# Two-token rows for the first loads, idle matmuls in planned waits, and last stores by SP

## The chip, the cores and the metric

One Trainium2 chip, one core of it. Its engines are TensorE (PE in the profiles, PEld for its weight loads), VectorE (DVE), ScalarE (ACT) and GpSimd (POOL); SP only issues transfers. A line of events gives start and length in us, the engine, the line of the kernel, the operation and what it writes and reads, and in brackets the engine's idle time before it and what ended it. The metric is the device time of one launch in microseconds (us), as the median of several runs. A profile of one launch gives a span, in nearly all launches some 1.7 to 2 us shorter than that launch's time because it counts from the first to the last instruction. A run over 1.5% above the fastest of the same kernel is called slow.

## The reference

A gated linear attention over 768 tokens (4 batches, 8 heads, head size 48), followed by an MLP over the 3,072 resulting rows of 384 values:

```python
f = 1.0 / (1.0 + np.exp(-f_logit))
for t in range(S):                                    # S = 768
    state = f[:, :, t, :, None] * state + np.einsum('bhd,bhe->bhde', k[:, :, t], v[:, :, t])
    y[:, :, t] = np.einsum('bhd,bhde->bhe', q[:, :, t], state)
x = y.transpose(0, 2, 1, 3).reshape(B * S, H * D)
h = x @ w_in                                          # 384 -> 2048
out = (h * sigmoid(h)) @ w_out                        # 2048 -> 384
```

## The kernel before

The sequence is cut into six chunks of 128 tokens. A *unit* is one chunk of one batch with all eight heads, so that there are 24 units, numbered (m, j): m is half a chunk (two batches), j one of the two batches. In a unit ScalarE makes Exp and Ln of f, TensorE the cumulative sum `cs` by a triangular matrix, ScalarE the factors `ia` and `a`, GpSimd `ki = k*ia`, VectorE `qg = q*a`. Then TensorE transposes both (`t_ps`), multiplies them (`a_ps`), VectorE masks (`atm`), and TensorE makes the outputs `y_ps` and the state update `d_ps`. The result, transposed, is `xT`, and the MLP (`h_ps`, then Silu to `hT`, then `o_ps`) runs on it.

Nothing is scheduled by hand. A small planner in the kernel simulates all engines with a duration for each task and writes the instructions out in the order that it finds. It is told how long a load takes, and how loads by SP and weights by GpSimd share the DMA engines while both run. What the planner believes decides the order of every engine, and that order is fixed before the launch.

```python
def load(m, j, name):                                 # one unit, one tensor: 128 tokens x 8 heads, rows of 48 fp32 = 192 B
    g, b = m // 2, m % 2 * HB + j
    t = ld.tile([C, H, D], F32, name=f"{name}_ld")    # 8 buffers
    src = SRC[name].rearrange("b h s d -> s (b h) d")[g * C:(g + 1) * C, b * H:(b + 1) * H]
    nc.sync.dma_start(out=t, in_=src)
# ...
def load_w_in(n):                                     # weights, fp32 to bf16 on the way, by GpSimd
    nc.gpsimd.dma_start(out=w_in_sb[:, :, n:n + 512], in_=w_in_src[:, :, n:n + 512])
# ... in the planner: idle matmuls, only ahead of the first MLP matmul
if e == "PE" and filler is not None and until in left:
    at = max(free.get(e, 0.0), 1.0)
    while start - at > 0.6:
        self.order.append((at, filler))
        at += 0.165 if at > 4.5 else 0.33
# ...
COPY, STORE = "ACT", "POOL"                           # all 24 stores by GpSimd
BEFORE = {0: ["ki1.0"]}                               # the first weights are issued behind ki of unit (1, 0)
SHARE = (0.25, 0.75)                                  # loads : weights while both flow, as the planner believes
```

The weights are 6.3 MB, and TensorE can do no MLP without their first piece. Idle matmuls (`w_ps`) multiply zeros; they are there to keep TensorE's clock up.

## Time and profile before

| | before |
|---|---|
| median of 3 runs, range | 204.23 us (203.98 to 205.19) |
| span of the profiled run, its TensorE clock | 203.2 us, 0.975 |
| first MLP matmul, last matmul | 22.25 us, 198.07 us |
| from the last matmul to the end | 5.1 us |
| half-clock stretches in the trace after 8 us | 12.2 to 15.6 and 70.3 to 77.1 us |

The order of events at the end:

```profile
198.15 0.48 ACT L424 COPY o_sb<-o_ps 128x384 f32<-128x384 f32 x1 [1.47 <-PE o_ps L418]
198.92 0.54 POOL L432 DMA_DIRECT2D out_dram<-o_sb  x1 [1.41 <-ACT o_sb L424]
```

The last copy ends at 198.63; GpSimd issues the store for 0.54 us and the span ends at 203.2.

### The profile page before, as it was taken

How to read it: one execution, taken by the hardware profiler on the slowest of the kernel's cores; microseconds unless marked ns; L12 is line 12 of the kernel's file. 1: busy time of each engine (PE TensorE's matmuls, PEld its weight loads, DVE VectorE, ACT ScalarE, POOL GpSimd, SP SyncE). 2: the span in 40 equal slices, each digit the busy share in tenths (PEclk: the TensorE clock that was granted, in tenths of full speed). 3: DMA queues.
4: the chain of work that ended last, by engine and by line, in shares of the span. 5: the costliest groups of instructions: out<-in, count | busy, mean ns of one | idle time of the engine just before them, and what ended most of it. 6: DMA issues, size and time to landing. Idle time of an engine off the chain costs nothing.

```text
span 203.2 us, 5048 instructions
## 1 busy us (share of the span) xinstructions
PE 186.7 (92%) x2076; PEld 139.1 (68%) x2076; DVE 112.5 (55%) x214; ACT 130.6 (64%) x244; POOL 59.0 (29%) x90
## 2 busy tenths in 40 slices
PE   7788899997999489979999999999999999999990
PEld 3445799554876258658768888667778889865650
DVE  3478650048784956589989940399999750000000
ACT  4446488646898664987798779996346568911110
POOL 5339600135241421192047110473520000012221
PEclk9979999999999959999999999999999999999999
DMA  7999999999999999999999997021110000002111
GB/s 133 187 187 167 170 188 184 197 194 286 189 184 209 214 182 188 180 225 217 175 198 220 205 176 110 2 79 42 39 54 27 3 0 3 0 30 75 68 69 71
DMA packets 105110, 27.06 MB, mean 133 GB/s; under 512 B 100352, under 2 KB 103936, under 8 KB 105088
## 3 DMA queue, kind: packets, MB, share of 16 engines
q1 hardware_dynamic: 99840, 18.88, 58.5%
q0 software_dynamic: 5248, 7.87, 16.2%
q8 instruction: 16, 0.26, 0.6%
q14 instruction: 6, 0.05, 0.1%
HBM read 25.17 MB, written 4.72 MB: 147 GB/s over the span
## 4 chain that ended last, share of the span: by engine, by line
PE 37%; issue 27%; DMA 12%; SPq 9%; DVE 7%; POOL 4%; ACT 2%; POOLq 0%; DVEq 0%; ACTq 0%
PE h_ps L403 14%; DMA q_ld<-in_q_dram 11%; PE o_ps L418 10%; SPq L227 9%; PE t_ps L312 3%; POOL out_dram L432 3%; PE h_ps L388 2%; PE a_ps L324 2%; DVE st L379 2%; DMA f_ld<-in_f_logit_dram 2%; DVE qg L288 2%; POOL ki L285 1%; PE y_ps L344 1%; DVE sd L376 1%; PE y_ps L340 1%
## 5 line engine op out<-in xcount | busy, mean ns | idle before, releaser
L418 PE MATMUL o_ps<-w_out_sb,hT 128*128 128x384 bf16 x384 | 68.4, 326 | 0.4 <-DMA w_out_sb<-in_moe_w_out_dram 0.4
L403 PE MATMUL h_ps<-xT,w_in_sb 128*128 128x256 bf16 x432 | 53.5, 279 | 0.0
L412 ACT ACTIVATE hT<-h_ps 128x512 bf16<-128x512 f32 x72 | 42.8, 597 | 16.3 <-PE h_ps L403 13.7
L418 PEld LDWEIGHTS <-hT 128*128 128x128 bf16 x384 | 36.0, 98 | 22.1 <-issue 0.6
L403 PEld LDWEIGHTS <-w_in_sb 128*128 128x128 bf16 x432 | 41.5, 100 | 6.0 <-issue 0.2
L285 POOL TENSOR_TENSOR ki<-k_ld,ia 128x384 bf16<-128x384 f32 x24 | 24.4, 1018 | 53.5 <-ACT ia L277 41.3
L288 DVE TENSOR_TENSOR qg<-q_ld,a 128x384 bf16<-128x384 f32 x24 | 21.3, 886 | 29.9 <-ACT a L282 18.8
L331 DVE TENSOR_TENSOR atm<-a_ps,triu 128x512 bf16<-128x512 f32 x48 | 30.9, 684 | 7.2 <-PE a_ps L324 6.9
L432 POOL DMA_DIRECT2D out_dram<-o_sb x24 | 13.6, 567 | 57.5 <-ACT o_sb L424 55.1
L424 ACT COPY o_sb<-o_ps 128x384 f32<-128x384 f32 x24 | 11.4, 477 | 23.4 <-PE o_ps L418 23.4
L291 POOL CAST vb<-v_ld 128x384 bf16<-128x384 f32 x22 | 12.9, 593 | 28.8 <-DMA v_ld<-in_v_dram 19.8
L277 ACT ACTIVATE ia<-cs 128x384 f32<-128x384 f32 x24 | 11.8, 492 | 11.4 <-PE cs L272 11.4
L388 PE MATMUL h_ps<-xT,w_in_sb 128*128 128x128 bf16 x288 | 17.7, 219 | 1.3 <-DVE xT L362 0.8
L317 DVE COPY qk<-t_ps 128x1024 bf16<-128x1024 bf16 x24 | 16.4, 682 | 4.4 <-PE t_ps L312 4.4
L258 ACT ACT_TABLE_LOAD x14 | 18.0, 1283 | 1.0 <-PEq L560 0.7
L388 PEld LDWEIGHTS <-w_in_sb 128*128 128x128 bf16 x288 | 16.4, 98 | 2.0 <-issue 1.0
L396 ACT ACTIVATE hT<-h_ps 128x512 bf16<-128x512 f32 x24 | 14.0, 597 | 5.1 <-PE h_ps L388 4.1
L351 DVE CAST y<-y_ps 128x384 bf16<-128x384 f32 x24 | 13.3, 554 | 7.2 <-PE y_ps L344 6.9
L265 ACT ACTIVATE f_ld<-f_ld 128x384 f32<-128x384 f32 x24 | 12.5, 522 | 6.1 <-DMA f_ld<-in_f_logit_dram 6.1
L379 DVE TENSOR_TENSOR st<-sd,al 48x192 bf16<-48x192 f32 x32 | 13.6, 425 | 0.8
L312 PE MATMUL t_ps<-ident,qg 128*128 128x128 bf16 x96 | 9.8, 226 | 3.6 <-DVE qg L288 3.5
L266 ACT ACTIVATE lf<-f_ld 128x384 bf16<-128x384 f32 x24 | 12.5, 523 | 0.8
(41 smaller groups left out, 182.2 us busy)
## 6 DMA issues: line engine op xcount, KB each, us to landing
f_ld<-in_f_logit_dram SPq DMA_DIRECT2D x24, 192.0 KB, 4.5
k_ld<-in_k_dram SPq DMA_DIRECT2D x24, 192.0 KB, 4.6
q_ld<-in_q_dram SPq DMA_DIRECT2D x24, 192.0 KB, 4.5
v_ld<-in_v_dram SPq DMA_DIRECT2D x24, 192.0 KB, 4.7
out_dram<-o_sb POOLq DMA_DIRECT2D x24, 192.0 KB, 2.2
w_in_sb<-in_moe_w_in_dram POOLq DMA_DIRECT2D x4, 384.0 KB, 8.3
w_out_sb<-in_moe_w_out_dram POOLq DMA_DIRECT2D x4, 384.0 KB, 16.4
```

Source lines behind the costliest of these rows:

```text
L227: nc.sync.dma_start(out=t, in_=src)
L258: nc.scalar.preload_act_table_set(tables[name])
L285: nc.gpsimd.tensor_mul(ki[m % 4][:, j, :, 0:D], loaded[m, j, "k"], ias[m, j])
L288: nc.vector.tensor_mul(qg[m % 4][:, j, :, 0:D], loaded[m, j, "q"], aas[m, j])
L317: nc.vector.tensor_copy(qkT[m, j], t_ps[m, j])
L331: nc.vector.tensor_mul(atm[m, j][:, r], att[m, j][:, r], triu[:, None, :].to_broadcast([C, NP, C]))
L379: nc.vector.tensor_mul(st[b][lo:lo + D, :, r * D:(r + 1) * D], src[lo:lo + D, :, r * D:(r + 1) * D], alast[m][lo:lo + D, j, :, None].to_br ...
L388: nc.tensor.matmul(h_ps[:, i], w_in_sb[:, kk, (n + i) * 128:(n + i + 1) * 128], xT[m][:, kk, j], start=(kk == 0), stop=(kk == KT - 1))
L403: nc.tensor.matmul(h_ps[:, i], w_in_sb[:, kk, (n + i) * 128:(n + i + 1) * 128], xT[m][:, kk].rearrange("p b c -> p (b c)"), start=(kk == 0 ...
L412: nc.scalar.activation(hT[m][:, n:n + 2, :], hs[m, n], AF.Silu)
L418: nc.tensor.matmul(os[m, j], hT[m][:, i, j * C:(j + 1) * C], w_out_sb[:, i, :], start=(i == 0), stop=(i == NT - 1))
L432: eng.dma_start(out=out[r0:r0 + C, :], in_=osb[m, j])
```

## The change

It has three parts. First, the loads of chunk 0 (m = 0 and 1) fetch two neighbouring tokens in one row of 384 B. Partition p then holds two tokens, 64 partitions are one batch, and a unit becomes half the heads of two batches; the cumulative sum, scores, outputs, updates and state are rewritten for that layout, and a unit now needs both loads of a pair. Second, idle matmuls may fill any wait that the planner foresees (over 0.4 us), not only those ahead of the MLP, as long as a buffer in PSUM, where TensorE writes its results, is free. Third, the last 8 stores are issued by SP and not by GpSimd. To make room, the other loads have six buffers and no longer eight. With new durations and ranks the planner also finds another order.

```diff
-            if e == "PE" and filler is not None and until in left:
+            if e == "PE" and filler is not None:
                 at = max(free.get(e, 0.0), 1.0)
-                while start - at > 0.6:
+                size, taken = self.pools["h"]
+                while start - at > self.slack:                       # 0.4
+                    if len(taken) >= size:
+                        if taken[-size] not in self.freed or self.freed[taken[-size]] > at:
+                            break
                     self.order.append((at, filler))
 ...
+    WIDE = (0, 1)
 ...
+        if m in WIDE:
+            if j == 0:
+                loaded[m, name] = singles.tile([C, H, 2, D], F32, name=f"{name}_w{m}")
 ...
+            src = SRC[name][b].rearrange("h (s i) d -> s h (i d)", i=2)[g * 64:(g + 1) * 64]
+            nc.sync.dma_start(out=loaded[m, name][64 * j:64 * (j + 1)].rearrange("p h i d -> p h (i d)"), in_=src)
+            return
 ...
+        if m in WIDE:                                                # cumulative sum: three matmuls for one
+            nc.tensor.matmul(dst, upto, src[:, 0:1].to_broadcast([C, 2, 4, D]), start=True, stop=False, ...)
+            nc.tensor.matmul(dst[:, 0], before, src[:, 1], start=False, stop=True, ...)
+            nc.tensor.matmul(dst[:, 1], upto, src[:, 1], start=False, stop=True, ...)
 ...
-        eng = {"ACT": nc.scalar, "POOL": nc.gpsimd, "SP": nc.sync}[STORE]
+        eng = nc.sync if m >= LATE else nc.gpsimd                    # LATE = 8
 ...
-                add(U(name, m, j), "LD", 1.07 + 1.5 * first, do(load, m, j, name), [user] if m >= 4 else [])
+            add(U(name, m, j), "LD", (0.78 if m in WIDE else 1.07) + 1.5 * first, do(load, m, j, name), ...)
 ...                                                                  # scores, outputs, updates, state: likewise rewritten
```

## The prediction

> **What bounds the kernel now.** I read the page first, then the busy time by stretch, the chain of waits, the order of events at the start and around the stalls.
>
> The page's 40 slices (5.08 us each; a digit is tenths busy):
>
> ```profile
> PE   7788899997999489979999999999999999999990
> PEclk9979999999999959999999999999999999999999
> DMA  7999999999999999999999997021110000002111
> ```
>
> The reader is to see three regimes. TensorE is full from slice 17 on; before that it has holes and two slices of reduced clock (slices 2 and 14, counted from 0); and the DMA engines are busy without a break until about 127 us. The same by stretch (length, then busy us and instruction count of each engine, clock, DMA share, GB/s):
>
> ```profile
> 0.00:22.25 22.25, 17.76 (x155) 9.90 (x155) 14.16 (x37) 10.78 (x21) 12.90 (x25) 0.92 1.22 168
> 22.25:41.55 19.30, 18.82 (x264) 15.68 (x264) 4.94 (x11) 13.16 (x22) 2.45 (x3) 1.00 1.21 184
> 41.55:100.00 58.45, 52.02 (x639) 39.36 (x640) 43.11 (x74) 43.85 (x83) 20.20 (x30) 0.94 1.12 205
> 100.00:198.07 98.07, 98.07 (x1022) 74.17 (x1019) 50.31 (x94) 62.32 (x118) 22.95 (x32) 1.00 0.37 76
> ```
>
> From 100 us to TensorE's last matmul at 198.07 nothing can be won except by less matmul work, and the change removes none. So time can come only from the fill (first MLP matmul at 22.25), from the stretch 41.55 to 100 (6.4 us idle and a clock of 0.94), and from the 5.1 us after the last matmul.
>
> The fill is paced by loads. In the order of events the loads follow each other on the SP queue every 1.05 us (0.99 us issue plus 0.04), and ScalarE begins on the four f tiles, loads 1, 5, 9 and 13, at 3.69, 7.91, 12.13 and 16.34: 4.22 us for four loads of 192 KB. Then the weights come, and the loads all but stop:
>
> ```profile
> 16.42 3.26 POOL L247 DMA_DIRECT2D w_in_sb<-in_moe_w_in_dram  x4
> 19.35 6.58 SPq L227 DMA_DIRECT2D q_ld<-in_q_dram  x1
> 22.25 1.51 PE L388 MATMUL h_ps<-xT,w_in_sb 128*128 128x128 bf16 x24 [0.53 <-DMA w_in_sb<-in_moe_w_in_dram]
> 25.98 5.72 SPq L227 DMA_DIRECT2D v_ld<-in_v_dram  x1
> 31.74 5.16 SPq L227 DMA_DIRECT2D f_ld<-in_f_logit_dram  x1
> 36.94 4.13 SPq L227 DMA_DIRECT2D k_ld<-in_k_dram  x1
> 40.93 0.56 DVE L288 TENSOR_TENSOR qg<-q_ld,a 128x384 bf16<-128x384 f32 x1 [10.79 <-DMA q_ld<-in_q_dram]
> ```
>
> Weights are issued at 16.42, once ki of the third unit is done, and the MLP starts at 22.25 on the first piece, 5.8 us later. While the 6.3 MB of fp32 weights flow (to about 41 us) a load takes some 5.5 us instead of 1.05. The q tile of chunk 1, issued at 19.35, is used at 40.93. This hurts little before the change, because TensorE has weights-paced MLP work of the first two unit pairs in that stretch.
>
> The third place to look is the largest hole:
>
> ```profile
> 66.78 2.22 DVE L379 TENSOR_TENSOR st<-sd,al 48x192 bf16<-48x192 f32 x2
> 67.33 1.00 POOL L285 TENSOR_TENSOR ki<-k_ld,ia 128x384 bf16<-128x384 f32 x1
> 69.64 0.40 PE L312 MATMUL t_ps<-ident,qg 128*128 128x128 bf16 x4 [2.06 <-DVE qg L288]
> ```
>
> Two state multiplies, 0.72 us elsewhere, took 2.22 us beside GpSimd's multiply; TensorE waited 2.06 us, and then ran slow: 12 matmuls of 256 columns took 2.67 us in the chain at 73.91, against 1.33 us at 91.44.
>
> **What the Trainium skill says.**
> - "DMA: Bandwidth & Descriptors", How a descriptor splits into AXI transactions: reads go in 256 B pieces from 256 B boundaries, 32 B beats; Why small descriptors are slow adds about 3 cycles per packet. A 192 B row then averages 9 beats plus 3 (the four alignments give 6, 12, 10, 8), a 384 B row 14 plus 3. Estimate: 17/(2 x 12) = 0.71 of the time, 1.05 x 0.71 = 0.75 us a load. No row of 384 B is in this trace.
> - "SBUF — State Buffer", Door 1: 64 partitions of one half reach 8 of the 16 ports. Each new load writes just 64 partitions, so if that binds, half of 435 GB/s gives 0.90 us (estimate). The planner's new number is 0.78, between the two. I take 0.78.
> - "DMA: Bandwidth & Descriptors", Queues, rings and completion order: each DMA engine takes turns between queues packet by packet. The trace agrees: 192 B rows lose badly to weight packets, 5.5 us against 1.05.
> - "TensorE: Matmul & The Clock Gate", Part 1: too little activity in a window of about 3.4 us halves the clock. The trace agrees: 12 matmuls at double time right after the 2.06 us hole.
>
> **The change part by part.**
>
> *Loads of chunk 0.* Sixteen loads at 0.78 instead of 1.05: 16 x 0.27 = 4.3 us less DMA time. But a unit is now half the heads of two batches, so both loads of a pair are needed: first f data at 3.69 - 1.05 + 2 x 0.78 = 4.2, later by 0.5. The third and fourth units need loads 9 and 10: 2.64 + 10 x 0.78 = 10.4 instead of 12.1 and 16.3.
>
> *Issue of the weights.* Still behind ki of the third unit. From 10.4: ScalarE now does both f pairs of Exp and Ln first (4 x 0.52), then ia (0.49), GpSimd ki (1.0), with 0.15 for hand-overs: 14.2 against 16.42, so -2.2. First weights 5.8 us later: MLP from 20.1.
>
> *What the new order puts into the weights' time.* Compared instruction by instruction, the new order on VectorE puts qg of chunk 1's first unit ahead of the masking of the last chunk-0 unit, and on TensorE its transposes after the second 24 MLP matmuls. Before, TensorE did all 192 MLP-in matmuls of chunk 0 and 36 MLP-out ones ahead of those transposes. So q and then v of chunk 1 are now needed while weights flow. First weight packets come about 1.6 us after issue, at 15.8; by then 16 x 0.78 = 12.5 us of loads from 1.65 are done, and 1.6 loads of chunk 1. The rest of k and all of q, 1.4 loads at 5.5 us and the about 3 us dead at the start of the weights, bring q to about 26.5 and v to about 32.5. TensorE would come to the transposes at about 24.4 (second weight piece), so it waits 3 us there and again for v: outputs of that unit at about 33.5, then a free run of 144 MLP matmuls (8.0 us) to 42. Counting finished matmul work at 0.0555 us per 128 columns and 0.1625 per 384 (chain: 36 in 2.01, 8 in 1.30), the new kernel at 42 has done about what the old one had at 40. The 4.3 us won are given back and 2 us more.
>
> *Stretch 42 to 100.* Here the old one loses some 12 us against its matmul work: idle, the halved clock, bubbles. At 42 the new one holds the hidden activations of three units instead of two and a reserve of 80 MLP-out matmuls (13 us), and the loads of the next units come 4 us earlier, so the holes at 48 to 51 should go. The hole at 66 comes from VectorE and GpSimd in each other's way and can come anywhere. I put the loss at 6 to 7 us, -5.5.
>
> *Extra matmul work.* Cumulative sums as three matmuls (0.33 for 0.165), scores as 16 instead of 8 (+0.33), outputs and updates with twice the columns (+0.25): 0.75 us x 4 units = 3 us, all in the fill, where TensorE waits. Idle matmuls go from 44 to 49, all but two before the MLP outputs begin; 5 x 0.165 us is nothing, and they cover planned waits only, not the wait for q.
>
> *Last stores by SP.* ScalarE's last copy ends at 198.63, GpSimd starts the store at 198.92, and GpSimd's own closing step from 198.90 is on the chain to 203.2. SP starts at once and GpSimd is finished long before: -0.8.
>
> Sum: +2 - 5.5 - 0.8 = -4.3; rounded for a better start still possible (a faster load lets q slip in ahead of the weights): 204.2 - 4.6 = 199.6.
>
> **The rivals.**
> - *The wait for q takes everything back.* For it: the 21.5 us that q took in the chain. If loads take 0.9 us, f comes 1.2 us later, q at 32, v at 37, and a hole over 3.4 us halves the clock: 203 to 206.
> - *The fill gain goes straight through.* If loads run at 0.75 or below, k and part of q are in before the weights, the hole vanishes, and 4.3 us of fill, the hole at 66 and the tail add up: 195 to 197. Against it: the old trace shows loads starved as soon as weights flow.
> - *Fill hidden anyway.* TensorE is 97% busy from 22 to 41 only because MLP follows weight pieces; if weights set that pace, the shift is that of their issue alone, 2.2 us, plus the tail: 201.
>
> **Range and chances.** The first part has an uncertainty of 3 us (arrival of q), the second of 3 us (how many holes stay), together about 4: 195.5 to 203.8. The 2% line is at 200.1, close to the middle, so faster and same are nearly even; slower than 208.3 needs both to go wrong.
>
> **What would show it.** f at ScalarE at 4.2 and chunk 0 landed by 15.5; weights issued near 14.2; MLP at 20; a VectorE wait for q of chunk 1 of some 2 to 4 us near 24 to 27 as the longest in the fill; at 100 us, less idle since 42; last matmul near 194; under 4.5 us after it. It is wrong if q is there in time, if a pair of loads takes 1.8 us or more, or if holes of the old size come back after 45.

## More of the kernel before

The main views stand in the prediction. Two more are used later. The first is the busy time in two stretches (length, then busy us and instruction count of PE, PEld, DVE, ACT and POOL, granted clock, DMA share, GB/s):

```profile
28.00:42.00 14.00, 13.52 (x174) 10.71 (x172) 2.09 (x5) 9.46 (x16) 0.99 (x2) 1.00 1.20 184
64.00:78.00 14.00, 10.56 (x98) 7.29 (x97) 8.56 (x15) 8.73 (x18) 4.04 (x6) 0.76 1.16 195
```

The reader is to see that TensorE is full and at full clock from 28 to 42 us, where weights flow, and that it loses time from 64 to 78 us, where it is busy for only 10.56 of 14 us and at a clock of 0.76.

## The result

The changed kernel took 201.94 us in the median of 4 runs (201.81 to 204.84) against 204.71 (203.98 to 205.21) for the kernel before in the same rounds. Ratios in this document are the mean time of one kernel's fast runs over that of the other's of the same rounds, so they aren't quite the ratio of the medians quoted; here it is 0.9857, with a 95% interval of 0.9814 to 0.9900.

The profiled launch of the changed kernel took 204.84 us and was slow, the other runs near 201.9. The profiled launch has a mean clock of 0.983, the fast ones have 0.991. The trace shows the half clock in pieces of 3.41 us, and each costs up to 1.7 us. The launch in the trace has two such pieces, and by their mean clocks the fast ones have one. That accounts for 1.7 of the 3.0 us between their spans (203.1 and 200.1); what makes the rest isn't shown.

The three slices of the page that answer to those in the prediction:

```profile
PE   7879757999989999989999999999999999999993
PEclk9999995799999999999999999999999999999999
DMA  5999999999999999899999900064111000002222
```

The holes of slices 13 and 14 are gone, and the low clock of slice 14 too. In their place are a hole in slice 5 and a low clock in slices 6 and 7, which is the weights' time. The same two stretches as before say how much each is:

```profile
28.00:42.00 14.00, 10.39 (x142) 9.64 (x139) 6.38 (x13) 3.72 (x7) 0.51 (x1) 0.76 1.22 186
64.00:78.00 14.00, 13.61 (x189) 10.71 (x188) 11.45 (x20) 11.18 (x20) 5.86 (x9) 1.00 1.03 220
```

The loss has moved: what was 10.56 us busy at a clock of 0.76 from 64 to 78 us is now 10.39 us busy at 0.76 from 28 to 42 us. The order of events shows where:

```profile
6.32 1.95 SPq L240 DMA_DIRECT2D f_w<-in_f_logit_dram  x2
13.42 0.52 ACT L296 ACTIVATE f_w<-f_w 128x384 f32<-128x384 f32 x1 [1.04 <-DMA f_w<-in_f_logit_dram]
16.87 3.25 POOL L271 DMA_DIRECT2D w_in_sb<-in_moe_w_in_dram  x4
20.73 6.00 SPq L245 DMA_DIRECT2D f_ld<-in_f_logit_dram  x1
23.36 1.51 PE L484 MATMUL h_ps<-xT,w_in_sb 128*128 128x128 bf16 x24 [0.44 <-DMA w_in_sb<-in_moe_w_in_dram]
31.10 0.56 DVE L325 TENSOR_TENSOR qg<-q_ld,a 128x384 bf16<-128x384 f32 x1 [3.77 <-DMA q_ld<-in_q_dram]
31.72 0.61 PE L358 MATMUL t_ps<-ident,qg 128*128 128x128 bf16 x4 [3.61 <-DVE qg L325]
32.55 2.77 PE L484 MATMUL h_ps<-xT,w_in_sb 128*128 128x128 bf16 x24
```

A pair of the new loads takes 1.95 us, so 0.98 each (by the records of the trace they land 0.98 us apart). Weights are issued at 16.87 and not earlier than before. While they flow, one old-style load takes 6 us. VectorE waits 3.77 us for q of chunk 1, TensorE 3.61 us behind it, and the 24 matmuls after that take 2.77 us instead of 1.51: the clock is halved from 30.8 to 37.6 us. The launch was slow, but the wait isn't a matter of the slow state: e_fill, below, profiled in the fast state, shows it too.

The end is shorter. The last copy starts at 199.86, 0.08 us after the last matmul, and the span ends 3.35 us after that matmul:

```profile
195.16 5.53 SPq L525 DMA_DIRECT2D out_dram<-o_sb  x3
199.86 0.48 ACT L519 COPY o_sb<-o_ps 128x384 f32<-128x384 f32 x1 [1.47 <-PE o_ps L514]
```

A sum over TensorE's records puts the fill (the time to about 40 us, while the weights come in) and the rest side by side. Each matmul is counted at its length when it runs back to back at full clock (0.0555 us for 128 columns of the MLP, 0.109 for 256, 0.1625 for 384; the small attention ones 0.02 to 0.06; idle ones 0). "Lost after 40" is the time from 40 us to the last matmul, less the work that was left. These totals are worked out from the traces and are not rows of a view; two-token kernels have 3.2 us more work, all of it before 40 us.

```
                          work in all  done by 40  left   40 us to last matmul  lost after 40
before                        166.0       21.8     144.2        158.1              13.9
after                         169.2       16.5     152.7        159.8               7.1
```

So at 40 us the changed kernel is 8.5 us behind (5.3 us less done, 3.2 us more to do), then it wins back 6.8 us. Up to 3.4 of these may be chance: the profile of the kernel before has two half-clock pieces in that stretch, and its launches have mean clocks from 0.967 to 0.992, so not all have as many. In the profiled launches the last matmul is later by 1.7 us, and the shorter end gives back 1.8.

### The profile page after: what moved, and what is told of

It reads as the page before. It is cut to its first block, busy times and chain, and to the rows that moved or that the text cites.

```text
span 203.1 us, 5142 instructions
## 1 busy us (share of the span) xinstructions
PE 188.3 (93%) x2121; PEld 142.2 (70%) x2121; DVE 114.8 (56%) x224; ACT 130.5 (64%) x246; POOL 56.3 (28%) x84
## 4 chain that ended last, share of the span: by engine, by line
PE 65%; DVE 10%; DMA 9%; SPq 8%; ACT 6%; issue 1%; DVEq 0%; ACTq 0%
PE o_ps L514 23%; PE h_ps L499 20%; DMA q_ld<-in_q_dram 9%; PE h_ps L484 7%; SPq L240 6%; PE t_ps L358 4%; DVE qg L325 4%; PE a_ps L381 3%; DVE states L475 2%; ACT L282 2%; PE x_ps L436 1%; SPq L245 1%; PE y_ps L415 1%; PE y_ps L411 1%; DVE qk L363 1%
## 5 line engine op out<-in xcount | busy, mean ns | idle before, releaser
L499 PE MATMUL h_ps<-xT,w_in_sb 128*128 128x256 bf16 x432 | 51.6, 273 | 0.4 <-ACT hT L508 0.3
L325 DVE TENSOR_TENSOR qg<-q_ld,a 128x384 bf16<-128x384 f32 x20 | 19.4, 971 | 30.8 <-ACT a L319 26.7
L322 POOL TENSOR_TENSOR ki<-k_ld,ia 128x384 bf16<-128x384 f32 x20 | 20.3, 1023 | 31.9 <-ACT ia L314 31.1
L392 DVE TENSOR_TENSOR atm<-a_ps,triu 128x512 bf16<-128x512 f32 x40 | 25.8, 686 | 3.0 <-PE a_ps L381 2.7
L525 POOL DMA_DIRECT2D out_dram<-o_sb x16 | 9.2, 577 | 38.5 <-PE o_ps L514 11.2
L484 PE MATMUL h_ps<-xT,w_in_sb 128*128 128x128 bf16 x288 | 19.1, 229 | 0.4 <-DMA w_in_sb<-in_moe_w_in_dram 0.4
L430 DVE CAST y<-y_ps 128x384 bf16<-128x384 f32 x20 | 11.1, 553 | 6.1 <-PE y_ps L415 5.8
L530 PE MATMUL w_ps<-zeros 128*128 128x384 bf16 x49 | 13.2, 397 | 1.2 <-DVE zeros L632 1.2
L475 DVE TENSOR_TENSOR states<-sd,al 48x192 bf16<-48x192 f32 x32 | 12.6, 394 | 0.9
L358 PEld LDWEIGHTS <-qg 128*128 128x128 bf16 x96 | 6.4, 99 | 7.8 <-DVE qg L325 6.8
## 6 DMA issues: line engine op xcount, KB each, us to landing
w_out_sb<-in_moe_w_out_dram POOLq DMA_DIRECT2D x4, 384.0 KB, 16.1
```

Of the source, the lines that this page charges most:

```text
L322: nc.gpsimd.tensor_mul(slots(m, ki[m % 4][:, j, :, 0:D]), flip(m, loaded[m, j, "k"]), slots(m, ias[m, j]))
L325: nc.vector.tensor_mul(slots(m, qg[m % 4][:, j, :, 0:D]), flip(m, loaded[m, j, "q"]), slots(m, aas[m, j]))
L358: nc.tensor.transpose(t[:, i, p, :], src[m % 4][:, j, 2 * p:2 * p + 2, :], ident)
L392: nc.vector.tensor_mul(atm[m, j][:, r], att[m, j][:, r], triu[:, None, :].to_broadcast([C, NP, C]))
L475: nc.vector.tensor_mul(st[b][lo:lo + D, :, r * D:(r + 1) * D], src[lo:lo + D, :, r * D:(r + 1) * D], alast[m][lo:lo + D, j, :, None].to_br ...
L484: nc.tensor.matmul(h_ps[:, i], w_in_sb[:, kk, (n + i) * 128:(n + i + 1) * 128], xT[m][:, kk, j], start=(kk == 0), stop=(kk == KT - 1))
```

## The experiments

All ran with the reference's inputs. Except the one marked wrong, all were correct.

| run | median (range), us | ratio to before, 95% | last matmul | done by 40 | lost after 40 | half clock after 8 us |
|---|---|---|---|---|---|---|
| changed kernel again | 203.54 (201.87 to 205.01) | 0.9961 (0.9917 to 1.0006) | | | | 31.0 to 37.8 |
| b_sp | 201.95 (200.24 to 203.43) | 0.9894 (0.9844 to 0.9945) | 196.6 | 22.5 | 13.1 | 71.1 to 74.6 |
| c_nowide | 200.47 (199.65 to 201.10) | 0.9838 (0.9802 to 0.9874) | 194.6 | 22.3 | 10.9 | none |
| d_truth | 204.00 (203.71 to 207.00) | 1.0007 (0.9970 to 1.0044) | 199.0 | 22.3 | 12.1 | 70.7 to 74.1 |
| h_oldidle | 201.59 (200.37 to 203.13) | 0.9898 (0.9852 to 0.9945) | 196.7 | 21.7 | 12.4 | 68.5 to 75.3 |
| e_fill | 202.23 (201.98 to 203.72) | 0.9949 (0.9910 to 0.9987) | 196.8 | 19.3 | 6.9 | none |
| f_full (wrong) | 197.54 (one run) | | 192.5 | 24.0 | 7.3 | none |
| i_late | 199.18 (198.73 to 200.10) | 0.9789 (0.9754 to 0.9824) | 193.7 | 22.1 | 6.6 | none |
| i_late2 | 207.50 (206.10 to 208.87) | 1.0148 (1.0097 to 1.0199) | 203.8 | 15.7 | 10.3 | 30.3 to 37.1 |
| k_clate | 202.23 (200.64 to 202.86) | 0.9904 (0.9856 to 0.9951) | 197.4 | 18.6 | 10.0 | none |
| j_two | 204.25 (203.47 to 205.46) | 1.0015 (0.9969 to 1.0061) | | | | 9.2 to 16.1 |
| l_act | 198.19 (197.94 to 199.49) | 0.9721 (0.9673 to 0.9769) | 192.9 | 22.6 | 6.3 | none |

"Half clock" is what the trace of the profiled launch shows, leaving out the last few microseconds after the work. The profiled launch of the changed kernel again was slow, its other runs fast; the profiled launches of the others were fast, that of f_full of unknown state. The ranges hold one more slow run each of b_sp (203.43) and d_truth (207.00). The rounds were not all on one chip: a_again, b_sp, c_nowide and d_truth ran together on chip 3, e_fill, f_full, h_oldidle and i_late on chip 15, i_late2, j_two and k_clate on chip 3 again, l_act on chip 4.

**The changed kernel again.** No edit.

> The changed kernel once more, for a profile in the fast state. Theory (the fill lost time to a wait for the q tile of chunk 1, the stretch to 100 us won it back, and the end of the program gave the rest): 201.9 us within 0.5, ratio 0.986; VectorE again waits 3 to 4 us for q before 31 us, the reduced clock lasts one window (about 3.4 us) instead of two, the last matmul ends near 196.8 instead of 199.8, and 3.3 us follow it. Rival (the slow profile differs somewhere else, not in the clock): the stretch 30 to 40 us shows the same work as in the slow profile.

The theory missed the time (201.9 within 0.5), and the profiled launch was slow once more. The gain came out at 0.4%, with an interval that reaches no change, against 1.4% in the first measurement. The two intervals (0.9814 to 0.9900 and 0.9917 to 1.0006) don't overlap, so rounds differ by more than the intervals say. The change is worth something between 0.4 and 1.4%. The wait, the half clock and their places repeat in the trace.

**The parts one by one.** b_sp is the kernel before with the last eight stores by SP and nothing else. c_nowide is the changed kernel without two-token rows, so the kernel before with the other two parts and the planner's new durations and ranks. h_oldidle is c_nowide with the old rule for idle matmuls.

```diff
 # b_sp, against the kernel before
-        eng = {"ACT": nc.scalar, "POOL": nc.gpsimd, "SP": nc.sync}[STORE]
+        eng = nc.sync if m >= 8 else nc.gpsimd
 # c_nowide, against the changed kernel (8 load buffers, one copy of v on ScalarE as before)
-    WIDE = (0, 1)
+    WIDE = ()
 # h_oldidle, against c_nowide
+            if e == "PE" and filler is not None and "I0.0.0" in left:
+                while start - at > 0.6:
```

> The kernel before with its last eight stores issued by SP and nothing else. Theory: the time from the last matmul to the end falls from 5.1 to 3.3 us, so 202.7 to 203.2 us, ratio 0.991, which is most of the whole gain of the change. Rival (the closing part is fixed, and the whole gain is made before the last matmul): 204.3 to 204.8, ratio 0.998 or more.

> The changed kernel with the two-token rows undone (chunk 0 loaded and computed as before, eight load buffers as before), the new rule for idle matmuls and the SP stores kept. Theory: the same as the SP stores alone within 0.5 us, 202.5 to 203.2, so that the rows are worth 0.5 to 1.3 us in all; the fill is that of before (MLP from about 22 us, no wait for q while weights flow), the holes after 45 us are those of before. Rival (rows are worth the whole gain, stores nothing): 204 or more. Rival (the idle matmuls carry the gain): 201.9 or less.

> The kernel with the rows undone (200.5 us), with the old rule for idle matmuls put back (only before the first MLP-in matmul, for planned waits over 0.6 us; 45 instead of 66). Theory (six idle matmuls that the new rule puts around the hole at 66 us keep the clock up): one window of halved clock comes back at about 70 us, 1.0 to 2.0 us slower, 201.5 to 202.5. Rival (what made the rows-undone kernel 1.5 us faster than the SP stores alone is the order that its planner's new durations give): 200.5 within 0.5, no halved clock.

The stores alone give 1.1% (about 2.2 us), somewhat more than the theory said. In the trace of b_sp the last matmul ends 3.3 us before the end, against 5.1 before, so 1.8 us of it is the shorter end. GpSimd issues nothing in the last part any more:

```profile
195.26 2.28 SPq L432 DMA_DIRECT2D out_dram<-o_sb  x2
196.71 0.48 ACT L424 COPY o_sb<-o_ps 128x384 f32<-128x384 f32 x1 [1.47 <-PE o_ps L418]
```

c_nowide missed its theory (202.5 to 203.2 us), and the rival that the idle matmuls carry the gain held; h_oldidle then came out as its theory said. The new rule for idle matmuls (66 instead of 45 in this kernel) takes the median from 201.59 to 200.47. They ran in different rounds, on different chips, and their intervals, 0.9802 to 0.9874 and 0.9852 to 0.9945, overlap a little, so the number, about 1.1 us, isn't firm. That h_oldidle stands where b_sp does (0.9898 and 0.9894) speaks against a gain from the new durations and ranks. The mechanism can be seen in the stretch from 64 to 78 us, first of h_oldidle, then of c_nowide:

```profile
64.00:78.00 14.00, 11.45 (x121) 8.28 (x120) 9.06 (x17) 8.46 (x18) 4.83 (x7) 0.76 0.99 202
```

```profile
64.00:78.00 14.00, 11.33 (x144) 8.93 (x143) 11.67 (x21) 9.57 (x19) 4.05 (x6) 1.00 0.99 202
```

TensorE is busy for about equally long, and it has a hole in front of the transposes in both (1.24 and 1.73 us), but with idle matmuls around that hole the clock stays at 1.00, and 23 more matmuls fit in, of which 8 are idle ones and 15 are work.

Most important: c_nowide, without the two-token rows, was faster than the changed kernel in the same rounds (200.47 against 203.54; the intervals don't overlap). So in those rounds the two-token rows, with the order that comes with them, cost 1.2%; against the changed kernel's first measurement, in other rounds, it would be 0.2%. In neither do they win anything.

**A planner that knows the measured rates.** The wait for q comes from an order that expects q earlier. d_truth tells the planner 0.98 us for the new loads and a lower share for loads beside weights, near what they got (in the changed kernel three of them landed between 21.5 and 41.3 us, 6.6 us each, which is 0.16 of the rate that they have alone).

```diff
-    SHARE = (0.25, 0.75)
+    SHARE = (0.145, 0.77)
-            add(U(name, m, j), "LD", (0.78 if m in WIDE else 1.07) + 1.5 * first, ...)
+            add(U(name, m, j), "LD", (0.98 if m in WIDE else 1.07) + 1.5 * first, ...)
```

> The changed kernel with two constants of its planner set to what the trace shows: 0.98 us for a load of chunk 0 (0.78 before) and 0.145 of the load rate for loads while weights flow (0.25 before, weights 0.77 for 0.75). The planner then puts the transposes of chunk 1 behind all MLP-in matmuls of chunk 0. Theory (the wait for q costs 3.6 us of TensorE and a window of halved clock, and is a matter of order alone): the wait and the halved clock vanish, 197.5 to 199.5 us. Rival (the early unit of chunk 1 is what filled the holes after 45 us, so that without it they come back): 201 to 204, with idle TensorE between 45 and 80 us as in the kernel before.

The theory missed and its rival held. There is no wait for q, and the work done by 40 us rises from 16.5 to 22.3 us. But the loss after 40 us rises from 7.1 to 12.1 us. The likely reason is that the MLP work that would have filled later holes has been used up in the weights' time. TensorE now waits for VectorE in the old place,

```profile
69.32 0.40 PE L381 MATMUL a_ps<-qk 48*128 48x128 bf16 x8 [2.06 <-DVE qk L363]
```

and a half-clock piece follows at 70.7. Truer durations make a different order, and not on their own a better one.

**Filling the wait for q.** e_fill puts 20 idle matmuls where TensorE waits for q.

```diff
     def transposes(m, j):
+        if (m, j) == (2, 0):
+            for _ in range(20):
+                warm()
```

> The changed kernel with 20 more idle matmuls (20 x 0.165 = 3.3 us) put where TensorE really waits for q, ahead of the transposes of chunk 1's first unit. Theory (that wait lets the clock be halved for one or two windows of 3.4 us afterwards): the granted clock stays 1.0 behind the wait, the MLP matmuls after it take 0.66 us per 12 instead of 1.3, and the runs lose their slow group: 199.5 to 201.5 us, 1.5 to 3 us less than the changed kernel (201.8 to 203.8 in its fast runs). Rival (the next wait, for v, hides what the clock costs): no change, 201.8 to 203.8.

```profile
27.60 3.42 PE L533 MATMUL w_ps<-zeros 128*128 128x384 bf16 x20
30.69 0.56 DVE L325 TENSOR_TENSOR qg<-q_ld,a 128x384 bf16<-128x384 f32 x1 [3.80 <-DMA q_ld<-in_q_dram]
```

The theory held for the clock and missed in the time, where its rival's range came. The wait for q stays as long as it was (3.80 us), the half clock after it is gone, and 2.8 us more work is done by 40 us than in the changed kernel (19.3 against 16.5). That is half of the 5.6 us by which i_late, below, is ahead at 40 us, so the halved clock would be one half of the damage and the wait itself the other. The time doesn't confirm it: the ratio, 0.9949, lies between the changed kernel's own two, and the fast launches of the changed kernel had the same span (200.1 us) with one half-clock piece as e_fill without any (200.2).

**Loads to all 128 partitions.** f_full replaces each pair of loads by a single one of the same bytes and the same rows of 384 B, written to 128 partitions at once. It fetches other tokens for the second half, so its result is wrong (relative error 0.41), with all else alike.

```diff
-            src = SRC[name][b].rearrange("h (s i) d -> s h (i d)", i=2)[g * 64:(g + 1) * 64]
-            nc.sync.dma_start(out=loaded[m, name][64 * j:64 * (j + 1)].rearrange("p h i d -> p h (i d)"), in_=src)
+            if j == 0:
+                src = SRC[name][b].rearrange("h (s i) d -> s h (i d)", i=2)[g * 64:g * 64 + 128]
+                nc.sync.dma_start(out=loaded[m, name].rearrange("p h i d -> p h (i d)"), in_=src)
```

> The changed kernel with each pair of chunk-0 loads (two of 196 KB, each to one half of the partitions) made one load of 393 KB of the same 384 B rows to all 128 partitions; the result is wrong on purpose (256 tokens of one batch instead of 128 of two). Theory (a load that writes one half of the partitions [...]measured 0.98 us a load): the pair takes 1.4 to 1.6 us instead of 1.95, and 16 loads' worth are in by 14 us instead of 18.4. Rival (the reads of HBM or the row itself bind): 1.9 to 2.0 us a pair as before.

The stretch from 8 to 14 us holds only loads, so its GB/s (the last number) are the rate of the loads. First the changed kernel, then f_full:

```profile
8.00:14.00 6.00, 4.48 (x56) 2.60 (x54) 3.35 (x6) 2.70 (x9) 3.17 (x4) 1.00 1.32 201
```

```profile
8.00:14.00 6.00, 5.24 (x67) 3.19 (x64) 4.68 (x6) 4.60 (x13) 3.50 (x4) 1.00 1.29 261
```

196.6 KB at 201 GB/s are 0.98 us, at 261 GB/s 0.75 us. The theory held: a pair's worth takes 1.5 us. Size of rows and bytes are the same in both, so what holds the changed kernel's loads at 0.98 us is most likely that each writes only half of the partitions. f_full also halves the number of transfers and reads other addresses; l_act, below, leaves both as they are and still gets a higher rate while it writes to both halves at once. With the faster loads the weights are issued at 15.07 instead of 16.87, the MLP starts at 21.75 instead of 23.36, q is there in time, no half clock appears, and the one run took 197.54 us.

**Weights one unit later.** i_late keeps the changed kernel and issues the weights behind ki of unit (1, 1), so that more loads of chunk 1 come in ahead of them. i_late2 goes one unit further. k_clate does to c_nowide what i_late does to the changed kernel.

```diff
 # i_late and k_clate; i_late2 has "ki2.0"
-    BEFORE = {0: ["ki1.0"]}
+    BEFORE = {0: ["ki1.1"]}
```

> The changed kernel with the weights issued one unit later, behind ki of the fourth unit instead of the third. Theory (q and v of chunk 1 wait because the weights start 2 to 3 us before their turn in the load queue): weights at about 18.5 us, q in the load queue ahead of them and no wait for q over 1 us, v still late; MLP from about 25 instead of 23.4; together 200.5 to 202.5. Rival (the weights' own arrival is the bound of the fill, whatever is loaded before): 1 to 2 us slower than the changed kernel, 203 to 205.5.

> The changed kernel with the weights issued behind ki of chunk 1's first unit, one step later again than in the run that gave 199.18 us. Theory (there q had landed before it was needed, so the order of loads and weights is settled): nothing more to win from loads, the MLP starts later by 2 to 3 us (27 us against 24.8) and TensorE waits for weights instead: 199.5 to 201.5 us. Rival (every load ahead of the weights still helps the stretch to 100 us): under 198.5 us.

> The kernel without two-token rows (new rule for idle matmuls and last stores by SP kept, 200.47 us), with the weights issued behind ki of the fourth unit instead of the third. Theory (late weights helped the changed kernel only because its order needs q of chunk 1 in the weights' time): this order puts 192 MLP-in matmuls ahead of the transposes of chunk 1 and so waits for weights, not for q; later weights move its MLP start from 22.3 to about 26 us and cost: 201.5 to 203.5 us. Rival (late weights are good of themselves, since more loads of chunk 1 land ahead of them): 198.5 to 200 us, and then the two-token rows have no part in what the best kernel so far wins.

In the order of events of i_late the weights are issued 1.5 us later than in the changed kernel, and yet all is better:

```profile
18.40 3.25 POOL L271 DMA_DIRECT2D w_in_sb<-in_moe_w_in_dram  x4
24.02 0.60 DVE L325 TENSOR_TENSOR qg<-q_ld,a 128x384 bf16<-128x384 f32 x1
24.83 0.84 PE L484 MATMUL h_ps<-xT,w_in_sb 128*128 128x128 bf16 x12 [0.48 <-DMA w_in_sb<-in_moe_w_in_dram]
```

The MLP starts at 24.83 instead of 23.36. But q of chunk 1 is used at 24.02, without a wait in the record, instead of 31.10; TensorE is busy for 13.96 of the 14 us from 28 to 42 us at a clock of 1.00, where it had 10.39 at 0.76:

```profile
28.00:42.00 14.00, 13.96 (x257) 13.61 (x254) 5.39 (x13) 9.76 (x17) 0.50 (x1) 1.00 1.26 188
```

Work done by 40 us rises from 16.5 to 22.1 us, and the loss after 40 us, 6.6 us, stays as low as in the changed kernel. The time is 199.18 us, under the range of its theory and 2.1% below the kernel before, with an interval across the 2% line (e_fill took 202.23 in the same rounds). One changed line of order gives what the two-token rows alone didn't.

One step further is too far. In i_late2 q is early too, but TensorE now runs dry for want of weights, falls to half clock for two pieces, and the time is 207.50 us, worse than its theory and its rival had expected:

```profile
32.21 1.46 PE L484 MATMUL h_ps<-xT,w_in_sb 128*128 128x128 bf16 x12 [3.80 <-DMA w_in_sb<-in_moe_w_in_dram]
```

And without two-token rows later weights cost: k_clate took 202.23 us, as its theory said, against 200.47 of c_nowide (in other rounds, with intervals that overlap a little). Its MLP starts at 26.50 instead of 21.21, and its order had no wait for q to save. So later weights are no gain of themselves; they mend the order of the two-token kernel. Compared at their better setting each, the kernel with two-token rows (i_late, 0.9789) is a little ahead of the one without (c_nowide, 0.9838), with intervals that overlap.

**Both halves at once, with a correct result.** A pair of loads can't be written as one transfer here, for it would need four dimensions, and the builder takes three. Two queues are the other way. j_two has GpSimd issue the second load of every pair, l_act has ScalarE issue the second load of the first four pairs; both have i_late's weights.

```diff
-            nc.sync.dma_start(out=loaded[m, name][64 * j:64 * (j + 1)].rearrange(...), in_=src)
+            eng = nc.gpsimd if j else nc.sync                       # j_two
+            eng = nc.scalar if (m, j) == (0, 1) else nc.sync        # l_act
+            eng.dma_start(out=loaded[m, name][64 * j:64 * (j + 1)].rearrange(...), in_=src)
```

> The kernel with weights one unit later (199.18 us), in which the second load of each two-token pair is issued by GpSimd instead of SP, so that the two loads, one for each half of the partitions, can run at the same time on two queues. The result stays correct. Theory (the 0.98 us a load come from writing to one half of the partitions at a time): with both halves written at once a pair takes 1.5 to 1.6 us instead of 1.95, the pairs of chunk 0 have landed by about 15 us instead of 18.4, the first weights and the first MLP matmul come 2 us earlier, and the time is 196.5 to 198.5 us. Rival 1 (two queues only take turns, the rows set the pace): a pair still takes 1.9 us and the time is 199 to 200. Rival 2 (GpSimd's issues, near 1 us each and eight of them, hold up its own ki and the pair's second halves): first ki and f later than 8 us and 5.6 us, time 200 to 203.

> The kernel with weights one unit later (199.18 us), in which the second loads of the first four two-token pairs (f, k, q, v of the first two units) are issued by ScalarE on its own hardware queue instead of by SP. Both queues then carry rows of 384 B in packets of one row, so they should take equal turns, and the two loads of a pair write to both halves of the partitions at once. The result stays correct. Theory (one half of the partitions takes no more than about 0.2 MB per us, both together 0.26): while both queues run, packets come at 640 to 690 per us instead of 524, the first eight loads have landed by 8.5 us instead of about 10.2, later loads and the first weights come 1 to 1.7 us earlier, and the time is 197.5 to 198.8 us. ScalarE, free again by about 6 us, costs at most 0.5 us of it. Rival 1 (queues take turns without running side by side): 524 packets per us as before, 199 to 200 us. Rival 2 (ScalarE is held by its issues past 7 us and the first Exp comes later): 200 to 202 us.

j_two failed as its second rival said. GpSimd was busy with its own memory fills and issued its first load at 4.44 us; beside SP's loads it then took 6.3 us to land, so the first f was used only at 10.72 instead of 5.60:

```profile
10.72 0.52 ACT L297 ACTIVATE f_w<-f_w 128x384 f32<-128x384 f32 x1 [8.64 <-DMA f_w<-in_f_logit_dram]
```

It showed two other things, both worked out from the records of the trace. While SP's queue wrote only one half of the partitions (to 9 us) its loads landed 1.12 us apart, and while GpSimd's queue wrote the other half (14 to 20 us, with little on SP's queue) its loads landed 1.12 us apart as well, although SP's queue moves packets of one row of 384 B and GpSimd's packets of 3,840 and 4,224 B, ten and eleven rows. One half of the partitions took 176 GB/s with either packets. And SP's queue nearly stood still beside GpSimd's, whose packets are ten to eleven times as large as its largest: from 15 to 18 us 172 packets of SP's queue and 132 of GpSimd's were moved, but 12.6 against 180 GB/s, and one SP load took 6.6 us to issue at 12.46.

l_act did what its theory said in the time: 198.19 us, the best correct kernel, 2.8% below the kernel before. In the rate it did so only in part. From 6 to 9 us, where both queues are full, the rate is 239 GB/s against 204 in i_late:

```profile
6.00:9.00 3.00, 2.85 (x25) 1.71 (x23) 0.00 (x0) 2.97 (x8) 1.09 (x2) 1.00 1.29 239
```

```profile
6.00:9.00 3.00, 2.74 (x24) 1.59 (x23) 0.00 (x0) 2.94 (x9) 1.01 (x2) 1.00 1.32 204
```

Over the whole time from 2 to 10 us it is only 215 against 200 GB/s. One reason is in the packet records: from 4 to 5 us one queue moved 159 of 204 GB/s and from 5 to 6 us the other 144 of 203, so that most bytes went to one half at a time. The weights are issued at 17.80 instead of 18.40, so of the expected 1 to 1.7 us only 0.6 came from there. In the sum over matmuls l_act is 0.5 us ahead of i_late at 40 us and loses 0.3 us less after it. That l_act is 1.0 us faster than i_late rests on runs of different rounds, with intervals that just overlap.

## Why the prediction was right or wrong

The time lies in the predicted range, 2.3 us above the predicted one in the first measurement, and at 203.54 us just inside it in the second. In part that is luck. The prediction expected 3.5 us from the rows and the new order (2 lost in the fill, 5.5 won after it) and 0.8 from the stores. The stores alone gave 1.1%, where the whole change gave 0.4 to 1.4%, and the rows gave nothing beside c_nowide. The mechanism was right where it foresaw the wait for q and the end of the later holes; it was wrong on the speed of the new loads, and there the prediction's own sign of being wrong, a pair of 1.8 us or more, came true. The total is better than its parts because large terms were off in opposite directions.

- *A load takes 0.78 us.* This step failed. It took 0.98 (pairs of 1.95), and f_full shows where it comes from: with all partitions the same rows take 0.75, which is the estimate from descriptors that the prediction worked out; with one half at a time they take 0.98. The prediction had both numbers, 0.75 and 0.90, and took a value between them, where the slower one sets the pace. And 0.90 itself was half of a peak rate; the measured row for 64 partitions in the Trainium skill, "SBUF — State Buffer", Door 1, has 196 GB/s (for 1 MiB), and that gives an estimate of 1.00 us, near what the trace shows (0.98 us, 201 GB/s).
- *f at 4.2, second f at 10.4, weights at 14.2, MLP at 20.1.* All follow from that number and came at 5.60, 13.42, 16.87 and 23.36. The front of the fill didn't move earlier at all (before: weights at 16.42, MLP at 22.25).
- *Chunk 1's q is needed while weights flow, TensorE waits 3 us for it.* Right in place and cause, and in size nearly: 3.77 us for VectorE, 3.61 for TensorE, but at 31.1 instead of 26.5. The first rival had given the numbers for loads of 0.9 us (q at 32, v at 37, and a halved clock), and in the fill it is what happened; v was used at 36.25.
- *At 42 us 2 us behind.* It was 8.5 at 40 us. Of that 3.2 are the extra matmuls (3 predicted), the rest the wait, its halved clock and the later front.
- *Stretch 42 to 100: 5.5 us won.* More: 6.8 us were won back from 40 us to the end. The holes and the halved clock near 70 us are gone, most likely because MLP work held back in the fill is there to fill them. d_truth speaks for the two being one trade: with more MLP work spent in the fill the wait there is gone, and the later holes return. But i_late has both gains, so the trade isn't forced. The rival's 203 to 206 us for the whole kernel didn't come in the first measurement and did in the second (203.54), so the time doesn't decide between them; the win after 40 us does. The last matmul, forecast near 194, ended at 199.8 in the profiled launch.
- *Last stores by SP: 0.8 us.* Mis-sized: the end got 1.8 us shorter in the changed kernel and in b_sp, which measured 2.2 us in all. By the records of the traces, the time from the end of the last copy to the landing of its store fell by 0.56 us (2.43 to 1.87), and that from the landing to the end by 1.22 (2.14 to 0.92): before, GpSimd's closing step ended only at 202.42, 1.36 us after the store that it had issued itself had landed at 201.06. The prediction named that step but made the gain too small.
- *Idle matmuls: nothing.* Probably wrong: on the order of c_nowide the new rule is worth about 1.1 us, by keeping the clock through the hole near 67 us. In the changed kernel they cover planned waits only, as predicted, and after the unplanned wait for q the clock is halved.
- *TensorE is full from slice 17 on.* A slip in reading: slice 17 has a 7, so it is from slice 18. Nothing rests on it.

What the prediction missed altogether is that the order of loads and weights was open to choice. i_late moves the weights one unit back, the wait vanishes, and the work done by 40 us and the gain after it come together.

What stays open: why the two measurements of the same change, 0.9857 and 0.9961, differ by more than their intervals (in the second, fast launches at an equal clock of 0.992 have spans from 201.0 to 202.1 us, so more than the clock varies); and how much activity TensorE needs in a window of 3.41 us to keep its clock, for the same kernel shows one half-clock piece in some launches and two in others.

## What to carry to other kernels

Here loads that fill half of the partitions at a time ran at 176 to 204 GB/s where the same rows to all partitions ran at 261, so ask which partitions a transfer writes before counting its rows, and let the slower of two estimates stand. When a fill gets faster or an order changes, ask which queue the next thing needed stands in: a load queued behind weights cost five times its time here, and in the changed kernel moving the weights one unit back was worth more than the new loads themselves. Work that TensorE could do early is also the reserve that fills its later holes, so a plan with no wait in the fill isn't by that the faster one.

## What the Trainium skill lacked or had wrong

- "SBUF — State Buffer", Door 1: the rate for 64 partitions, 196 GB/s in its table, agrees (201 GB/s); the asymptote in the same row, about 218 GB/s and half of the peak, was not reached with loads of 197 KB. It lacks that loads alternating between the two halves on one queue (0.98 us each) are a little faster than loads that all go to one half (1.12 us, 176 GB/s).
- "SBUF — State Buffer", "Can I just issue two DMAs to hit both halves?": it says that two at once gain only 6%. Over 2 to 10 us of l_act the gain is 7% (215 against 200 GB/s), which agrees; in the 3 us with both queues full it is 17% (239 against 204), which is more than the page allows for.
- "DMA: Bandwidth & Descriptors", Queues, rings and completion order: turns are taken by packets, "≈9-17 descriptors typical". Here GpSimd's queue packed 10 to 11 rows of 384 B, and SP's and ScalarE's queues one. Beside the weights, whose packets are recorded with 768 and 1,024 B, SP's rows of 192 B took 5 to 6 us a load instead of 1.05. That section doesn't say that the queues differ in this, and for SP's and ScalarE's queues on this chip the page gives no packet size.
- "TensorE: Matmul & The Clock Gate", Part 1: the length of the window agrees (pieces of 3.41 us), but the page has the clock fall after an idle window, and here a hole of 2.06 us with smaller ones beside it was enough for two pieces, another of 2.06 us with idle matmuls on both sides (d_truth) was followed by one, and one of 1.73 us with idle matmuls on both sides (c_nowide) brought none. How busy a window must be isn't given.
- No page that I read says that GpSimd's closing step outlasts the landing of a store that it issued, here by 1.36 us: with that store on GpSimd the end took 5.1 us after the last matmul, with SP 3.35.
